# The last product of a seven-product matmul, in column halves on two banks, and the last rows stored in halves

## The chip, the core and the metric

The kernel runs on one core of one Trainium2 chip. The metric is device time in microseconds of one execution; a figure for a kernel is the median of its runs. Five engines work side by side from queues of their own: TensorE (PE; its weight loads are listed as PEld), VectorE (DVE), ScalarE (ACT), GpSimd (POOL) and SyncE (SP), which here issues the stores and the transposing DMAs.

## What is computed

Attention with a sliding window and a linear bias, and behind it a two-layer network with an ELU, in one program:

```python
# q, k, v: (8, 8, 576, 64); w_in: (512, 2048); w_out: (2048, 512)
scores = q @ k^T / 8 - slope[h] * |i - j|     # kept where 0 <= i - j < 128
attn = softmax(scores)
x = (attn @ v) as (4608, 512)                 # tokens x (heads * head_dim)
h = x @ w_in
g = where(h > 0, h, exp(min(h, 0)) - 1)       # ELU
out = g @ w_out                               # (4608, 512), float32
```

## The kernel before

**Stages.** The 4,608 tokens are cut into nine blocks of 512 (`NTB = 9`), and these into 18 pairs `n` of 256 tokens. A schedule written out by hand (`manual_schedule`, slots numbered `s`, dictionaries `early`, `HID`, `tasks`, `OUT`, `late`) fixes the order in which each engine's instructions are issued. In each slot the attention of a later batch, a piece of the hidden layer (`hidden`: 8 matmuls for 256 tokens, two activations on ScalarE; `elu`: one operation on VectorE) and a piece of the output layer follow one another.

**The output layer.** From pair 2 of the 18 on (`SEVEN`, n = 1 to 17) the product of `g` (256 tokens x 2048) with `w_out` (2048 x 512) is not computed as eight block products but as seven, with sums and differences of blocks on VectorE (the scheme of Strassen and Winograd). Rows are cut in two halves of 128, columns in two of 256, the inner dimension in two of 1024. `T[1..4]` are differences of blocks of `w_out`, made once; `sums(n, i)` makes the four sums `S1..S4` of blocks of `g`; `product(n, i)` for i = 1 to 7 is eight accumulating matmuls of 128x128 weights with 256 columns. Products share accumulators in PSUM: of the two banks of a pair, `z` takes 1, then 6, 7 and 4 on top of each other, `x` takes 2 (read together with the copy of product 1), and 5 and then 3. So after product 7 bank `z` holds P1+P6+P7, which ScalarE copies to the SBUF tile `U7` (`kept(n, 7)`), and after product 4 it holds the lower left block of the result.

**Finishing a pair.** `combine` makes three of the four 128x256 blocks with an addition on VectorE (`add`, line 354): C11 is the copy `U1` plus product 2, C12 is `U6` plus product 3 on product 5, C22 is `U7` plus `U5`. The lower left block is bank `z` after product 4, copied by ScalarE (line 398). `put` (line 412) issues the store of a row tile `tile_out(n, i)` (128 rows x 512 columns of float32, tag `ob`) on SyncE's queue: row tile 0 after C12, row tile 1 after C22, 256 KB each.

**The last pair.** n = 17 has no hidden layer beside it any more. Its products run in slots `s = 15 + 8*17` and `s + 1`, with bank `sp2` as `z`, and in the order 1, 2, 6, 5, 7, 3, 4. After product 7 and 3 come C22 (its store takes columns 256 to 512 of row tile 1) and C12 (the store of the whole of row tile 0), then product 4, and then `last_out`: ScalarE copies columns 0 to 128 of bank `sp2` and issues their store on its own queue, VectorE copies columns 128 to 256 and SyncE issues theirs (line 417 the copies, 412 the stores). The banks `hp0` and `hp1`, in which the hidden layer is accumulated, are not used after the last `elu` (line 323).

**Where a store's completion is waited for.** Each store or transposing DMA that SyncE or ScalarE issues counts up one of eight completion semaphores, which are taken in turn. At the end of the program SyncE waits for each of the eight in order of their numbers before the closing barrier.

Of the kernel before, what the change touches and what calls it, by code (L numbers as in the profile page):

```python
# [18 lines left out]
def kernel(  # L19
# [9 lines left out]
    nc = tc.nc  # L29
    B, H, S, D = q.shape  # L30
    NTOK, DO = out.shape
    FF = moe_w_in.shape[1]
    NFC = FF // 128
    NTB = NTOK // 512
# [3 lines left out]
    V = nc.vector  # L38
# [10 lines left out]
    def one(shape, dt, name):  # L49
        return const.tile(shape, dt, name=name, tag=name)  # L50
# [5 lines left out]
    T = [None] + [one([128, 8, 256], F16, f"T{i}") for i in (1, 2, 3, 4)]  # L56
# [21 lines left out]
    hp = [ps_h.tile([128, 512], F32, name=f"hp{i}", tag=f"hp{i}") for i in range(2)]  # L78
# [70 lines left out]
    with tc.manual_schedule():  # L149
# [199 lines left out]
        def A(n, i, k):  # L349
            c = 256 * (n % 2) + 128 * i  # L350
            return gs[n // 2][:, 8 * k:8 * k + 8, c:c + 128]

        def add(o, a, b, op=ALU.add):
            V.tensor_tensor(out=o, in0=a, in1=b, op=op)  # L354
# [16 lines left out]
        def place(n, i):  # L371


            z, x = XY[n] if n < 2 * NTB - 1 else (sp[2], sp[3] if i == 2 else sp[0])
            return (z if i in (1, 4, 6, 7) else x)[:, 0:256]

        def kept(n, i):
            if (n, i) not in U:
                U[n, i] = work.tile([128, 256], F32, name=f"U{i}", tag=f"U{i}", bufs=1)
            return U[n, i]  # L380

        def tile_out(n, i):
            if (n, i) not in obs:
                obs[n, i] = work.tile([128, DO], F32, name="ob", tag="ob")
            return obs[n, i]
# [12 lines left out]
                nc.scalar.copy(tile_out(n, 1)[:, 0:256], o)  # L398

        def combine(n, what):  # L400
            if what == "C11":
                add(tile_out(n, 0)[:, 0:256], kept(n, 1), place(n, 2))
            elif what == "C12":
                add(tile_out(n, 0)[:, 256:512], kept(n, 6), place(n, 3))
                put(n, 0, 0, DO)
            else:
                add(tile_out(n, 1)[:, 256:512], kept(n, 7), kept(n, 5))
                put(n, 1, 0 if n < 2 * NTB - 1 else 256, DO)

        def put(n, i, c0, c1, queue=nc.sync):  # L410
            r = 256 * n + 128 * i
            queue.dma_start(out[r:r + 128, c0:c1], tile_out(n, i)[:, c0:c1])

        def last_out(n):
            o = place(n, 4)
            for c0, copy, queue in ((0, nc.scalar.copy, nc.scalar), (128, V.tensor_copy, nc.sync)):
                copy(tile_out(n, 1)[:, c0:c0 + 128], o[:, c0:c0 + 128])
                put(n, 1, c0, c0 + 128, queue)

        wz = fore[4][:, 0:256]  # L420

# [69 lines left out]
        early, tasks, late, HID, OUT = {}, {}, {}, {}, {}  # L491

        def at(s, f, *a):
            tasks.setdefault(s, []).append((f, a))

        def at_once(s, f, *a):
            tasks.setdefault(s, []).insert(0, (f, a))

        def after(s, f, *a):
            late.setdefault(s, []).append((f, a))  # L500
# [130 lines left out]
        for n in SEVEN:  # L631
            s = 15 + 8 * n
            ps = (19, 20, 21, 22, 23, 25, 27, 29, 30) if n == 1 else range(s, s + 9)
            if n < 2 * NTB - 1:
                for d, i in ((-1, 1), (1, 2), (3, 3), (4, 4)):
                    (at_once if n > 2 else at)(ps[d] if d > 0 else ps[0] - 1, sums, n, i)
                after(ps[2], combine, n, "C11")
                after(ps[6], combine, n, "C12")
                (at_once if n > 2 else at)(ps[8], combine, n, "C22")
                for d in range(8):  # L640
                    OUT[ps[d]] = [(product, (n, i, j, j + 1)) for i, j in turns[7 * d:7 * d + 7]]
            else:
                at_once(s - 3, sums, n, 3)
                for i in (2, 1):
                    at_once(s - 2, sums, n, i, 0, 6)
                    at_once(s - 1, sums, n, i, 6, 8)
                at(s - 1, product, n, 1)
                OUT[s] = [(product, (n, 2)), (combine, (n, "C11")), (sums, (n, 4)), (product, (n, 6)), (product, (n, 5))]
                OUT[s + 1] = [(product, (n, 7)), (product, (n, 3)), (combine, (n, "C22")), (combine, (n, "C12")),
                              (product, (n, 4)), (last_out, (n,))]  # L650


        SOFT = {15 + 8 * n + d for n in SEVEN[1:] for d in (0, 1, 2, 3, 4, 7)} | set(range(11, 19)) | {20, 22, 23} | set(range(16 * NTB - 10, 16 * NTB + 8))
# [45 lines left out]
```

The softmax here doesn't subtract the row's maximum and nothing guards it: scores larger than these inputs give would overflow.

## Time and profile before

| | |
|---|---|
| median of three runs | 311.28 us (310.63 to 312.19) |
| span of the profiled execution, first to last instruction | 308.9 us |
| time of the profiled execution outside its span | not given on the page; the median is 2.4 us above the span |
| granted TensorE clock, mean | 0.998 |
| PE busy | 300.1 us, 97% of the span, 4071 matmuls |
| DVE busy / ACT busy | 257.5 us (83%) / 241.8 us (78%) |
| the chain that ended last: PE / DVE / DMA / ACT / POOL | 72% / 8% / 6% / 5% / 4% |
| stores on SyncE's queue | 35 of 256 KB, 2.2 us from issue to landing (median) |

Times are microseconds from the first instruction. The profile has one row for each instruction; the timeline merges neighbours of one kind, and gives a start, a length, the engine, the line, the operation, the tiles written and read, and in brackets the idle time ahead of it with what ended that. A matmul's end is modelled, and matmuls overlap: the spacing of their starts is what eight of them cost.

### The profile page before, as it was taken

To read this page: it belongs to the slowest core of one execution; us is meant where nothing else is said; L and a number is where in the kernel's file an instruction comes from. 1 tells how busy PE (TensorE), PEld (TensorE's weight loads), DVE (VectorE), ACT (ScalarE), POOL (GpSimd) and SP (SyncE) were. 2 spreads that over 40 slices of the span, in tenths; PEclk is the share of its full clock that TensorE was granted. 3 is DMA by queue.
4 is the path that set the end of the run, shared out by engine and by line. 5 is a ranking of instruction groups with operands and counts; after the bars stand their busy time and mean duration, and the time that the engine had idled before them with its cause. 6 is when DMAs were issued, how large, how long until landed. Compare 5 with 4: busy or idle time off the path is not lost.

```text
span 308.9 us, 9820 instructions
## 1 busy us (share of the span) xinstructions
PE 300.1 (97%) x4071; PEld 256.1 (83%) x4071; DVE 257.5 (83%) x498; ACT 241.8 (78%) x446; POOL 108.4 (35%) x163
## 2 busy tenths in 40 slices
PE   6899999999999999999999999999999999999995
PEld 4788875798888888988888888888899888898884
DVE  4646888988989998997989998989998788886782
ACT  4576678678798788878887889778888897968871
POOL 8937867273252315141616061706000001010000
PEclk9999999999999999999999999999999999999999
DMA  9999999999194919395969896999530202030103
GB/s 96 196 197 202 201 180 185 94 118 115 21 165 63 169 35 161 43 152 59 132 70 138 110 102 78 138 124 122 60 94 7 91 17 87 19 98 0 70 28 110
DMA packets 96509, 32.04 MB, mean 104 GB/s; under 512 B 83920, under 2 KB 91984, under 8 KB 96464
## 3 DMA queue, kind: packets, MB, share of 16 engines
q0 software_dynamic: 75920, 18.36, 64.2%
q1 hardware_dynamic: 20400, 12.98, 17.1%
q8 instruction: 32, 0.52, 0.7%
q14 instruction: 13, 0.11, 0.1%
q10 hardware_dynamic: 144, 0.07, 0.1%
HBM read 36.70 MB, written 9.44 MB: 149 GB/s over the span
## 4 chain that ended last, share of the span: by engine, by line
PE 72%; DVE 8%; DMA 6%; ACT 5%; POOL 4%; issue 4%; POOLq 0%; DVEq 0%
PE hp L305 33%; PE op L393 13%; PE av L393 12%; DMA VP<-in_v_dram 4%; PE spa L225 3%; PE spa L271 3%; DVE g L323 3%; POOL e L316 2%; PE sp L393 2%; ACT e L315 2%; DMA s<-in_q_dram 2%; ACT EX L236 1%; PE sp L253 1%; POOL VP L114 1%; DVE xn L260 1%
## 5 line engine op out<-in xcount | busy, mean ns | idle before, releaser
L305 PE MATMUL hp<-xT,wi 128*128 128x256 f16 (+3 forms) x1488 | 144.2, 245 | 1.0 <-DVE g L323 0.5
L305 PEld LDWEIGHTS <-wi 128*128 128x128 f16 x1600 | 119.9, 98 | 18.1 <-issue 6.3
L323 DVE SCALAR_TENSOR_TENSOR g<-e,hp 128x512 f16<-128x512 f32 x138 | 93.7, 679 | 22.2 <-ACT e L313 12.5
L316 POOL TENSOR_SCALAR e<-e 128x512 f32<-128x512 f32 x44 | 28.0, 636 | 158.8 <-ACT e L315 152.9
L312 ACT ACTIVATE e<-hp 128x512 f32<-128x512 f32 x98 | 58.6, 597 | 28.5 <-PE hp L305 23.1
L313 ACT ACTIVATE e<-e 128x512 f32<-128x512 f32 x100 | 63.1, 631 | 3.2
L393 PEld LDWEIGHTS <-S 128*128 128x128 f16 x544 | 51.2, 98 | 6.7 <-issue 0.6
L393 PEld LDWEIGHTS <-g 128*128 128x128 f16 x408 | 38.2, 98 | 4.7 <-issue 0.6
L241 DVE TENSOR_TENSOR EX<-EX,TAB 128x1024 f16<-128x1024 f16 x48 | 32.9, 686 | 6.2 <-ACT EX L236 4.0
L114 POOL DMA_DIRECT2D VP<-in_v_dram x40 | 34.6, 878 | 0.6 <-PE hp L305 0.3
L315 ACT ACTIVATE e<-hp 128x512 f32<-128x512 f32 x40 | 24.1, 601 | 10.9 <-PE hp L305 10.9
L393 PE MATMUL op<-T,S 128*128 128x256 f16 x200 | 30.0, 273 | 0.1
L233 ACT ACTIVATE EX<-spa 128x1024 f16<-128x1024 f32 x24 | 24.6, 1025 | 3.7 <-PE spa L225 3.4
L393 PE MATMUL av<-T,S 128*128 128x256 f16 x176 | 26.4, 273 | 0.1
L236 ACT ACTIVATE EX<-sp 128x512 f16<-128x512 f32 x48 | 26.0, 596 | 0.0
L354 DVE TENSOR_TENSOR S<-g 128x1024 f16<-128x1024 f16 (+2 forms) x35 | 23.5, 671 | 0.8 <-PE op L393 0.2
L393 PE MATMUL op<-wo,g 128*128 128x256 f16 x128 | 19.2, 272 | 0.1
L393 PE MATMUL av<-wo,g 128*128 128x256 f16 x120 | 18.0, 272 | 0.0
L277 DVE TENSOR_TENSOR xn<-spa,rden 128x512 f16<-128x512 f32 x24 | 16.6, 692 | 0.8
L108 POOL DMA_DIRECT2D st<-in_k_dram x24 | 16.2, 686 | 2.8 <-DMA s<-in_q_dram 1.9
L108 POOL DMA_DIRECT2D st<-in_q_dram x24 | 15.9, 666 | 0.6 <-DMA VP<-in_v_dram 0.6
L271 PE MATMUL spa<-VP,EX 128*128 128x65 f16 x336 | 15.4, 193 | 0.1
(139 smaller groups left out, 379.3 us busy)
## 6 DMA issues: line engine op xcount, KB each, us to landing
out_dram<-ob SPq DMA_DIRECT2D x35, 256.0 KB, 2.2
VP<-in_v_dram POOLq DMA_DIRECT2D x32, 128.0 KB, 5.7
st<-in_k_dram POOLq DMA_DIRECT2D x24, 144.0 KB, 5.2
st<-in_q_dram POOLq DMA_DIRECT2D x24, 144.0 KB, 5.9
wi<-in_moe_w_in_dram POOLq DMA_DIRECT2D x4, 512.0 KB, 10.7
wo<-in_moe_w_out_dram POOLq DMA_DIRECT2D x4, 512.0 KB, 10.1
VP<-in_v_dram POOLq DMA_DIRECT2D x8, 64.0 KB, 5.8
s<-in_k_dram POOLq DMA_DIRECT2D x1, 512.0 KB, 12.1
```

Of the source, the lines that this page charges most:

```text
L108: nc.gpsimd.dma_start(st[b][32 * g:32 * g + 32, w, :, :, :, :].rearrange("p h n j d -> p (h n) (j d)"), (q, k)[w][b, 2 * g:2 * g + 2, :, : ...
L114: nc.gpsimd.dma_start(VP[b % 2][0:p, n, :, 0:D], v[b, :, 128 * n:128 * n + p, :].rearrange("h p d -> p h d"))
L236: nc.scalar.activation(unit(b, u)[:, g, :, :], sp[g].rearrange("p (h c) -> p h c", h=2), AF.Exp, scale=0.125)
L241: V.tensor_tensor(out=e, in0=e, in1=TAB[:, int(u == 3), 2 * gp:2 * gp + 2, :, :], op=ALU.mult)
L271: nc.tensor.matmul(a[:, h // 4, h % 4, :], ex_[u][:, c:c + 128], VP[b % 2][:, n, h, 0:D + 1], start=j == 0, stop=j == len(parts) - 1)
L305: nc.tensor.matmul(p[:, l * w + u0:l * w + u1], w_in_sb[:, c, fc * 128:(fc + 1) * 128], xT[:, c, x0:x0 + u1 - u0], start=(c == 0), stop=(c ...
L312: nc.scalar.activation(e[:, 0:n], p[:, 0:n], AF.Relu, scale=-1.0)
L313: nc.scalar.activation(e[:, 0:n], e[:, 0:n], AF.Exp, scale=-1.0)
L315: nc.scalar.activation(e[:, 0:n], p[:, 0:n], AF.Exp)
L316: nc.gpsimd.tensor_scalar(out=e[:, 0:n], in0=e[:, 0:n], scalar1=1.0, scalar2=0.0, op0=ALU.min, op1=ALU.max)
L323: V.scalar_tensor_tensor(out=gs[t][:, f0:f0 + nf, c0:c0 + w], in0=sh(es.pop((t, c0, f0))), scalar=1.0, in1=sh(hps.pop((t, c0, f0))), op0=A ...
L393: nc.tensor.matmul(o, a[:, j, :], b[:, j, :], start=j == 0 and i in (1, 2, 5), stop=j == 7, skip_group_check=True)
```

## The change

It does three things. First, product 4 of the last pair no longer accumulates on bank `sp2`: it goes to `hp0` and `hp1`, each 128 columns wide, eight matmuls for the first half and then eight for the second. Second, VectorE adds each half to the same columns of `U7`, the copy of P1+P6+P7 that exists for C22 already, and writes the result tile; the first half's store is issued by ScalarE, the second's by SyncE. Third, for the last two pairs (n = 16 and 17, `late`) each 256 KB store is replaced by two of 256 columns, issued as soon as their block is there. The output is the same sum.

```diff
         def combine(n, what):
+            late = n >= 2 * NTB - 2
             if what == "C11":
                 add(tile_out(n, 0)[:, 0:256], kept(n, 1), place(n, 2))
+                if late:
+                    put(n, 0, 0, 256)
             elif what == "C12":
                 add(tile_out(n, 0)[:, 256:512], kept(n, 6), place(n, 3))
-                put(n, 0, 0, DO)
+                put(n, 0, 256 if late else 0, DO)
             else:
                 add(tile_out(n, 1)[:, 256:512], kept(n, 7), kept(n, 5))
-                put(n, 1, 0 if n < 2 * NTB - 1 else 256, DO)
+                if n == 2 * NTB - 2:
+                    put(n, 1, 0, 256)
+                put(n, 1, 256 if late else 0, DO)
...
         def last_out(n):
-            o = place(n, 4)
-            for c0, copy, queue in ((0, nc.scalar.copy, nc.scalar), (128, V.tensor_copy, nc.sync)):
-                copy(tile_out(n, 1)[:, c0:c0 + 128], o[:, c0:c0 + 128])
-                put(n, 1, c0, c0 + 128, queue)
+            for half, queue in enumerate((nc.scalar, nc.sync)):
+                c, o = slice(128 * half, 128 * half + 128), hp[half][:, 0:128]
+                for j in range(8):
+                    nc.tensor.matmul(o, A(n, 1, 1)[:, j, :], T[4][:, j, c], start=j == 0, stop=j == 7)
+                add(tile_out(n, 1)[:, c], kept(n, 7)[:, c], o)
+                put(n, 1, 128 * half, 128 * half + 128, queue)
...
                 OUT[s + 1] = [(product, (n, 7)), (product, (n, 3)), (combine, (n, "C22")), (combine, (n, "C12")),
-                              (product, (n, 4)), (last_out, (n,))]
+                              (last_out, (n,))]
```

## The prediction

> **What bounds the kernel now.** I read the page first. TensorE is busy for nearly the whole span, so work that is moved beside it is worth nothing, except where TensorE has already ended.
>
> ```profile
> span 308.9 us, 9820 instructions
> PE 300.1 (97%) x4071; PEld 256.1 (83%) x4071; DVE 257.5 (83%) x498; ACT 241.8 (78%) x446; POOL 108.4 (35%) x163
> ```
>
> The change touches only the last two pairs, so I went to the end of the chain that ended last (start, length, what):
>
> ```profile
> 303.75 0.87 PE spa L393 x8
> 304.62 0.89 PE sp L393 x8
> 305.51 0.02 issue
> 305.53 0.27 ACT ob L417
> 305.81 0.02 issue
> 305.83 0.29 DVE ob L417
> ```
>
> TensorE leads it up to 305.51. Then the two copies of the last block stand one behind the other, although they are on two engines. The timeline of the same stretch shows why the second is late, and what follows it:
>
> ```profile
> 304.19 0.43 DVE L354 TENSOR_TENSOR ob<-U,U 128x256 f32<-128x256 f32 x1 [1.93 <-ACT U L396]
> 304.46 1.04 PE L393 MATMUL sp<-T,g 128*128 128x256 f16 x8
> 304.64 1.84 SPq L412 DMA_DIRECT2D out_dram<-ob  x3
> 304.66 0.42 DVE L354 TENSOR_TENSOR ob<-U,spa 128x256 f32<-128x256 f32 x1
> 305.53 0.27 ACT L417 COPY ob<-sp 128x128 f32<-128x128 f32 x1 [1.38 <-PE sp L393]
> 305.83 0.37 ACTq L412 DMA_DIRECT2D out_dram<-ob  x1
> 305.83 0.29 DVE L417 COPY ob<-sp 128x128 f32<-128x128 f32 x1 [0.75 <-ACT ob L417]
> ```
>
> VectorE's copy was released by ScalarE's copy (0.75 us idle, "<-ACT ob L417"), not by TensorE: both read bank `sp2`, and the program lets them do so in turn only. SyncE's last store is issued behind VectorE's copy; its row by itself starts at 306.15 and takes 0.33. From there to the end of the span (308.89) are 2.74 us in which no compute engine works. The list of DMAs says that 1.6 of these are that store's way to its landing:
>
> ```profile
> out_dram<-ob SPq DMA_DIRECT2D x1, 64.0 KB, 1.6
> ```
>
> The rest is SyncE's closing waits and the barrier. SyncE's rows for the program's end in the stretch 307.85 to 308.1 are these, the last two lines:
>
> ```profile
> L694 SPq EVENT_SEMAPHORE  x3: 27/28/28, 307.9 to 308.0; - x3
> L694 SPq DRAIN  x1: 13/13/13, 308.1 to 308.1; - x1
> ```
>
> In all there are nine such waits between 306.5 and 308.0. The one at 307.8 is where the last store's landing was noticed; behind it three more semaphores were still looked at, which had long been full, at about 0.06 us each (307.87, 307.93, 307.99), and only then the drain began.
>
> **Product 4 in halves.** It removes 8 matmuls of 256 columns (1.04 us with the last one's 0.272 of latency, so (1.04 - 0.272) / 7 = 0.110 each) and adds 16 of 128 columns, each with a weight load. The same shapes run in the hidden layer early in the trace:
>
> ```profile
> 27.80 0.99 PEld L305 LDWEIGHTS <-wi 128*128 128x128 f16 x17
> 27.86 1.06 PE L305 MATMUL hp<-xT,wi 128*128 128x128 f16 x16
> ```
>
> One such matmul's row is 0.219 long, so the spacing is (1.06 - 0.219) / 15 = 0.056, though a weight load's row is 0.098: consecutive loads overlap. With the first matmul at 304.46 as now, half 0 ends at 304.46 + 7 x 0.056 + 0.219 = 305.07, and half 1 at 304.46 + 15 x 0.056 + 0.219 = 305.52, against 305.50 now: **+0.02**. The banks cost no wait: the last reading of `hp0` is an `elu` that ended at 300.35, and U7's copy (303.79 to 304.16) is over before the product starts. The bounds for the spacing are 0.056 and 0.098 (no overlap of the loads); I take 0.056, since that row has the very shape.
>
> The Trainium skill speaks against this step: its page "TensorE: Matmul & The Clock Gate", section "Back-to-back issue gap", gives a sustained spacing of about 81 ns for a pair of weight load and matmul of 128 columns. By it, as an estimate, half 1 would end 15 x 0.025 = 0.38 us later than in my sum and nearly all of the gain below would go. The trace's sixteen in 1.06 us contradict it here.
>
> **The adds.** Each is a VectorE addition of 128 columns of float32, one operand from PSUM; the trace has none of that size. Above lies the same addition with 256 columns (0.42), below ScalarE's copy of 128 columns (0.27). VectorE's copy of 128 columns out of PSUM is the nearest row, 0.29. Multiplications of float32 from PSUM (L260 and L277 groups) take 0.425 at 256 columns and 0.692 at 512, 1.04 ns a column, and 0.42 - 128 x 0.00104 gives 0.29 again; I take that. Half 0's add is ready at 305.07, as C12's add ends (304.66 + 0.42 = 305.08), runs 305.11 to 305.40, and is covered by half 1 on TensorE; ScalarE's store goes out at 305.43 instead of 305.83. ScalarE now waits for VectorE there, with nothing queued behind it. If the cover were gone (C12's add 0.15 us later), the second add would start to slip.
>
> Half 1's add starts as ScalarE's copy did, 0.03 after TensorE (305.55), for the two halves lie in two banks and, by the program's waits, it waits for TensorE alone; not for half 0's store, though both write one tile. It ends at 305.84, and SyncE issues 0.03 later, at 305.87 instead of 306.15: **-0.28**. SyncE is free then: C12's store is issued at 305.11 as now and takes 0.34. Bounds of this term: -0.30 with an add of 0.27, -0.15 with one of 0.42.
>
> **Stores in halves.** SyncE gets three more issues of 0.33 each. Pair 16's first half goes out after its C11 add (ends at 292.04), its row tile 1 in two issues near 300.7 and 301.4, pair 17's C11 half right behind, near 301.7. SyncE then waits for C22 until 304.64 anyway, with nothing else queued: **0**. The buffer that C22 of pair 17 writes is that of pair 16's row tile 0, whose last half is issued at 299.78 as now and has 4.4 us until 304.19, against 2.2 to land. Without that slack, the C22 add would wait, and C12's store behind it. What changes at the end is that 128 KB fewer are on their way behind 305.1. The last store lands 1.6 us after its issue, like ScalarE's before it, so I see no queueing to save: **0**, with -0.1 as the other end.
>
> **The order of the closing waits.** The three additional DMAs turn the round of eight semaphores by three: by the program's waits the last store, now on the fifth of the eight, gets the eighth. SyncE looks at them in order, so the three looks behind the landing (3 x 0.06) move ahead of it, into time in which it waits anyway: **-0.18**, between -0.18 and 0.
>
> **Sum.** -0.28 - 0.18 = -0.46 against the profiled span, which becomes 308.9 - 0.46 = 308.4 (its TensorE end at 305.52, last issue at 305.87). The 2.4 us outside the span (311.28 - 308.9) are not touched, so the median of the runs goes from 311.28 to 310.82.
>
> **Rivals.** *Half the gain*: the add costs 0.42 as the 256-column one does, or the closing waits stay where they are; then -0.15 - 0.18 = -0.33 or -0.28, that is 310.95 to 311.0. For it speaks that neither row is in the trace.
>
> *Weight loads become the bound* (the slower side): sixteen loads with 128 columns each instead of eight with 256. If at this place a pair takes the 0.098 of a load row, half 1 ends 15 x 0.042 = 0.63 later, and the sum is -0.46 + 0.63 = +0.17, 311.45. It decides from a spacing of 0.056 + 0.46 / 15 = 0.087. Against it are all groups of this shape in the trace, at 0.056 and with TensorE at the same clock.
>
> *The second add waits for the first half's store*, because of the shared result tile. Then it starts at 305.43 + 1.6 = 307.03, the last issue comes at 307.35, and the total is +1.2 - 0.18 = +1.0, 312.3. The listed waits speak against it.
>
> *It doesn't do what it says*: were the end set by another store, nothing would move, 311.28. C12's 256 KB landed 2.0 after 305.11, at 307.1, well ahead of the last one at 307.8, so this is unlikely.
>
> **How the numbers follow.** Forecast (-0.40 to -0.56) 0.60; half the gain 0.20; loads as the bound 0.08; waiting for the store 0.04; nothing moves 0.08. None of the cases reaches 0.5% of the time (1.56 us, about what a measurement of this kernel can tell from no change); such a result would need something that no row here shows, or runs that scatter: the three given lie 0.65 below and 0.91 above their median. I give 0.06 to faster, 0.05 to slower, 0.89 to within. The range goes from 310.82 - 0.65 = 310.2 up past the slower rival (311.45) to 311.7; the store rival at 312.3 is left out, with the tails.
>
> **What would show it.** In the changed profile: sixteen matmuls into `hp` in about 1.06 us from the same distance to C12's add; two adds of 0.29, the first ending before TensorE does, the second 0.03 behind it; SyncE's last issue 0.33 to 0.37 after TensorE's end instead of 0.65; and no look at a semaphore between the last landing and the drain. A spacing over 0.08, an idle time before the second add that ends with a DMA, or a last store that lands in more than 1.8 would each prove me wrong.

## The result and the profile after

The changed kernel takes 310.11 us (median of 16 runs, 309.48 to 310.72). The kernel before, run beside it, takes 310.89 (16 runs, 309.96 to 312.19), 0.39 less than the median of three that the forecast started from. The ratio is 0.9977 (0.9968 to 0.9987): 0.7 us faster, with an interval from 0.4 to 1.0, and within 0.5%. The forecast time of 310.82 was too high, and the measured one lies 0.09 us below the stated range of 310.2 to 311.7. The direction was right, and so was that the change stays within 0.5%; the forecast difference of 0.46 lies in the interval.

The chain that ended last, in the changed kernel (start, length, what):

```profile
304.36 0.87 PE spa L393 x8
305.23 0.91 PE hp L423 x16
306.14 0.02 issue
306.16 0.29 DVE ob L354
```

Where two copies stood in turn there is one addition. The timeline of the same stretch (line 423 are the matmuls in `last_out`, 417 the stores):

```profile
304.80 0.42 DVE L354 TENSOR_TENSOR ob<-U,U 128x256 f32<-128x256 f32 x1 [1.92 <-ACT U L396]
304.96 0.99 PEld L423 LDWEIGHTS <-g 128*128 128x128 f16 x16
305.07 1.06 PE L423 MATMUL hp<-T,g 128*128 128x128 f16 x16
305.27 0.42 DVE L354 TENSOR_TENSOR ob<-U,spa 128x256 f32<-128x256 f32 x1
305.71 0.29 DVE L354 TENSOR_TENSOR ob<-U,hp 128x128 f32<-128x128 f32 x1
306.03 0.37 ACTq L417 DMA_DIRECT2D out_dram<-ob  x1
306.16 0.29 DVE L354 TENSOR_TENSOR ob<-U,hp 128x128 f32<-128x128 f32 x1 [0.16 <-PE hp L423]
```

Sixteen matmuls of 128 columns take 1.06 us, where eight of 256 took 1.04. The first add is done before TensorE ends; the second is released by TensorE (0.16 idle) and by nothing else. SyncE's rows of the program's end, in the stretch 308.02 to 308.2, where before three more looks at semaphores came behind the landing:

```profile
L701 SPq DRAIN  x2: 7/10/13, 308.1 to 308.2; - x2
L701 SPq EVENT_SEMAPHORE  x1: 28/28/28, 308.0 to 308.0; - x1
```

The wait at 308.0 is the one that ends with the last store's landing, and the drain follows at once.

Yet both profiled spans are 308.9 us. The product starts at 304.46 in the one and at 305.07 in the other: this execution of the changed kernel was 0.61 late when it came to the last pair. VectorE's instructions, compared one by one, run within 0.01 of each other up to 4 us, are 0.61 apart at 8.4 us, and 0.61 apart again at the last pair; from 16 us on the distance stays within 0.04 of 0.62, except from 111 to 114 us (up to 0.86). So what the change does is read in the tail, which I measure from the start of C22's add of the last pair to the end of the span, in single rows of the traces. Each figure is from one profiled execution:

| | before | after | difference | forecast |
|---|---|---|---|---|
| product 4's start to the last store's issue | 1.69 | 1.41 | -0.28 | -0.28 |
| issue to the landing noticed | 1.66 | 1.56 | -0.10 | 0 |
| landing noticed to the end | 1.08 | 0.90 | -0.18 | -0.18 |
| C22's add to the end (C22 to product 4 is 0.27) | 4.70 | 4.14 | -0.56 | -0.46 |

### The profile page after: what moved, and what is told of

Its sections match the earlier page's. It is cut to its first block, busy times and chain, and to the rows that moved or that the text cites. A ratio compares the mean times of both kernels' runs of the same rounds, so it can differ in the third digit from the quotient of the medians.

```text
span 308.9 us, 9842 instructions
## 1 busy us (share of the span) xinstructions
PE 300.8 (97%) x4079; PEld 256.5 (83%) x4079; DVE 258.0 (84%) x499; ACT 241.5 (78%) x445; POOL 108.5 (35%) x163
## 4 chain that ended last, share of the span: by engine, by line
PE 76%; DVE 7%; ACT 6%; DMA 5%; issue 3%; POOL 2%; POOLq 0%; DVEq 0%; ACTq 0%
PE hp L305 34%; PE op L393 13%; PE av L393 12%; PE spa L225 4%; PE spa L271 3%; DVE g L323 2%; DMA s<-in_q_dram 2%; DMA VP<-in_v_dram 2%; ACT EX L236 2%; PE op L329 1%; DMA xT<-xn 1%; PE sp L393 1%; POOL e L316 1%; PE sp L305 1%; ACT e L315 1%
## 5 line engine op out<-in xcount | busy, mean ns | idle before, releaser
L393 PEld LDWEIGHTS <-g 128*128 128x128 f16 x400 | 37.4, 98 | 4.6 <-issue 0.6
```

Of the source, the lines that this page charges most:

```text
L393: nc.tensor.matmul(o, a[:, j, :], b[:, j, :], start=j == 0 and i in (1, 2, 5), stop=j == 7, skip_group_check=True)
```

## The experiments

Theory: three separate terms, as in the table. Rivals: the adds carry the whole gain; or the landing term is no term at all, but scatter of one profiled execution. The ratios of the first four are of whole runs, against 35 further runs of the kernel before; their intervals reach half a microsecond and more to each side, so the verdicts rest on the tails, one profile for each run.

### The adds alone

```diff
 # kernel before, with last_out of the changed kernel; puts as before
-                              (product, (n, 4)), (last_out, (n,))]
+                              (last_out, (n,))]
```

> The kernel before with product 4 in halves and the two adds alone; all stores as before. I measure the tail, from the start of C22's add of the last pair to the end of the span: 4.70 us before, 4.14 after (-0.56). First theory, three separate terms (adds -0.28, the round of semaphores -0.18, the landing of the last store -0.10): the adds alone take 0.28 off between product 4's start and the last issue (1.69 to 1.41), the three looks behind the landing stay, and the store lands 1.6 to 1.7 after its issue: tail 4.42, time -0.28. Rival, that the adds carry the whole gain (the last store lands earlier because ScalarE's goes out earlier): tail 4.14 to 4.3, time -0.5 or more.

Measured: ratio 0.998 (0.9964 to 0.9996), tail 4.54. Product 4 to the last issue is 1.41, as forecast, and the three looks behind the landing are still there (1.08 from landing to end). But the landing came 1.78 after the issue. The list of DMAs of the last stretch of this run, and then that of the changed kernel (KB each, issue to landing):

```profile
out_dram<-ob SPq DMA_DIRECT2D x1, 256.0 KB, 2.0
out_dram<-ob ACTq DMA_DIRECT2D x1, 64.0 KB, 2.0
out_dram<-ob SPq DMA_DIRECT2D x1, 64.0 KB, 1.8
```

```profile
out_dram<-ob SPq DMA_DIRECT2D x1, 128.0 KB, 1.7
out_dram<-ob ACTq DMA_DIRECT2D x1, 64.0 KB, 1.7
out_dram<-ob SPq DMA_DIRECT2D x1, 64.0 KB, 1.5
```

Counted from C22's add, the 256 KB of row tile 0 move until 2.59. ScalarE's store is issued at 1.24, and its packets start at 2.44, 1.20 later, where in the changed kernel they start 0.90 after the issue; the last store's start 0.96 later instead of 0.83. Neither theory had this: issued earlier, the last stores run into row tile 0. The whole-run times do not decide here: the interval, 0.1 to 1.1 us faster, holds the theory's 0.28 and the rival's 0.5, and the median of 310.06 is as low as that of the whole change (310.11), though this tail is 0.40 longer.

### The stores in halves alone

```diff
 # changed kernel, with last_out and product 4 of the kernel before
-                              (last_out, (n,))]
+                              (product, (n, 4)), (last_out, (n,))]
```

> The changed kernel with the end of the kernel before: product 4 on the shared bank, two copies in turn; only the stores of the last two pairs are in halves. First theory: product 4's start to last issue stays at 1.69; the last store has the eighth semaphore, so no look lies between landing and drain (-0.18), and with 128 KB fewer on the way it lands 0.10 earlier: tail 4.42, time -0.28. Rival, that the halves of the stores are worth nothing: tail 4.70, time within 0.1.

Measured: ratio 1.0004 (0.9986 to 1.0021), tail 4.43: 1.69 to the issue, 1.58 to the landing, 0.90 to the end. The number is the theory's 4.42; the reason given for 0.10 of it is not, as the next run shows.

### The round of semaphores alone

```diff
 # kernel before
-                put(n, 0, 0, DO)
+                if n == 15:
+                    put(n, 0, 0, 256)
+                put(n, 0, 256 if n == 15 else 0, DO)
...
-                put(n, 1, 0 if n < 2 * NTB - 1 else 256, DO)
+                if n in (14, 15):
+                    put(n, 1, 0, 256)
+                put(n, 1, 256 if n in (14, 15, 17) else 0, DO)
```

> The kernel before with three earlier 256 KB stores (row tile 1 of pair 14, both row tiles of pair 15) issued as two halves one right behind the other, so that the round of eight semaphores turns by three and the last store gets the eighth; everything from pair 16 on as before. First theory: the looks at semaphores behind the landing move ahead of it, tail 4.70 - 0.18 = 4.52, landing as before, time -0.18. Rival, that the order of the looks costs nothing because the barrier waits for something else: tail 4.70, time unchanged.

Measured: ratio 0.9992 (0.9972 to 1.0013), tail 4.43, better than the 4.52 expected. Landing to end is 0.90 (-0.18, as forecast). Here row tile 0 is whole, and yet the last store lands 1.57 after its issue. So 256 KB on the way do not delay a last store that is issued as late as in the kernel before, and the 1.66 of the first profile was not their doing.

### One turn too many

```diff
 # changed kernel: pair 15's row tile 0 in halves as well
-                put(n, 0, 256 if late else 0, DO)
+                if n == 15:
+                    put(n, 0, 0, 256)
+                put(n, 0, 256 if late or n == 15 else 0, DO)
```

> The changed kernel with one more earlier store in halves (row tile 0 of pair 15), so that the last store gets the first of the eight semaphores and ScalarE's the eighth. First theory: SyncE waits for the last landing first and only then looks at the seven others, about 0.06 each: tail 4.14 + 7 x 0.06 = 4.57, time +0.43 against the change, so about -0.13 against the kernel before. Rival (the order costs nothing): tail 4.14, time as with the change.

Measured: ratio 1.0 (0.9979 to 1.002), tail 4.58 (+0.44, forecast +0.43). SyncE's rows in its stretch 307.4 to 308.0:

```profile
L703 SPq EVENT_SEMAPHORE  x8: 28/28/28, 307.4 to 307.9; - x8
L703 SPq DRAIN  x2: 7/10/13, 307.9 to 308.0; - x2
```

The landing is noticed by the first of these eight; the other seven are looked at behind it, one each 0.06 us, and then comes the drain. A store that is split far upstream, whose bytes nobody waits for, takes most of the change's gain away.

### A second base, for repeats

The remaining runs have TensorE transposes and a ScalarE copy in place of SyncE's 31 transposing DMAs. The last pair is the same, and seven early stores are split so that the round of semaphores stands as in the kernel before. Neither the kernel before nor the changed kernel was profiled a second time as it stands.

```diff
 # kernel before
-            if copy is None:
-                nc.sync.dma_start_transpose(out=xT[:, :, o:o + n], in_=x[0:n, :])
-                return
...
-                at(a + 3, turn, b, u)
+                at(a + 3, turn, b, u, nc.scalar.copy, sp[3])
...
+                if 3 <= n < 10:
+                    put(n, 0, 0, 256)
```

> A base for the next runs: the kernel before with its 31 transposing DMAs replaced by TensorE transposes and a ScalarE copy (nothing of it in the last pair), and with seven early stores split, so that the round of eight semaphores stands as before. Its time differs upstream (31 x 4 transposes more on TensorE: some us slower than the kernel before). What counts is the tail, from C22's add of the last pair to the end. If the tail is fixed by the program: 4.70 as before, with the last store landing 1.66 after its issue. Rival, that the landing scatters between executions by some 0.1: 1.57 as in the variants whose last store had the eighth semaphore, tail 4.61.

> The base once more, for the scatter of the tail. The two profiles with this end of the program so far gave 4.70 and 4.62, the whole difference between the last packet of the last store and its landing (0.45 and 0.38). If that part scatters: 4.60 to 4.72 again, product 4 to last issue 1.69 exactly, looks behind the landing three.

> The whole change on the base with TensorE transposes. If the gain is what the tail shows: tail 4.14 (within 0.03), and about 0.56 less time than the base. Rival, that the change also takes something off before the tail: same tail, but 1 us or more less time than the base.

> The change on that base once more: tail 4.14 to 4.20, product 4 to last issue 1.41 exactly, no look behind the landing.

The base takes 375.19 us (373.03 to 377.62), 64 more than the kernel before, where I had written "some us"; why it is so much I did not pursue. With the change it is 373.94 (373.25 to 375.13), 1.25 less; that is what the rival asked for (1 us or more), but with runs of one kernel up to 4.6 us apart it decides nothing about half a microsecond. The tails do: 4.62 and 4.61 for the base, 4.18 and 4.12 with the change. The means differ by 0.47. Term by term: to the last issue 1.69 and 1.69 against 1.41 and 1.41; issue to landing 1.59 and 1.58 against 1.55 and 1.55; landing to end 1.08 and 1.08 against 0.95 and 0.90. In the repeat of the base, the two copies in turn:

```profile
368.60 0.27 ACT L416 COPY ob<-sp 128x128 f32<-128x128 f32 x1 [1.37 <-PE sp L390]
368.90 0.29 DVE L416 COPY ob<-sp 128x128 f32<-128x128 f32 x1 [0.75 <-ACT ob L416]
```

and in the repeat of the change the second add:

```profile
368.23 0.29 DVE L351 TENSOR_TENSOR ob<-U,hp 128x128 f32<-128x128 f32 x1 [0.16 <-PE hp L422]
```

On this base the landing term is thus 0.03, not 0.10. From the last store's last packet to the noticed landing it takes 0.47 and 0.48 in the traces of the kernel before and of the adds alone, and 0.37 to 0.40 in the other nine with a last store of this size on one queue. On the first base the two long ones are the two whose last store has the fifth semaphore, but on the second base the fifth goes with 0.37 and 0.39, so the semaphore alone does not make it. Whether this part scatters between executions or belongs to the program of the first base stays open, and with it 0.07 of the 0.56 in the table.

### Row tile 0 whole

```diff
 # change on the second base; pair 17's row tile 0 in one store behind C12
-                if late:
+                if n == 2 * NTB - 2:
                     put(n, 0, 0, 256)
...
-                put(n, 0, 256 if late else 0, DO)
+                if 3 <= n < 11:
+                    put(n, 0, 0, 256)
+                put(n, 0, 256 if 3 <= n < 11 or n == 16 else 0, DO)
```

> The change on that base, but row tile 0 of the last pair is stored whole (256 KB) behind C12's add as before; one more early store is split, so that the last store keeps the eighth semaphore. First theory: the two last stores meet the 256 KB on the DMA engines, as in the run with the adds alone: ScalarE's packets begin 1.20 instead of 0.90 after their issue, the last store lands 1.70 to 1.78 after its issue instead of 1.56, tail 4.24 to 4.35. Rival, that bytes on the way do not matter: tail 4.14.

Measured: tail 4.24, landing 1.67 after the issue, a little under the 1.70 expected, against 1.55 with the change. The list of DMAs of the last stretch:

```profile
out_dram<-ob SPq DMA_DIRECT2D x1, 256.0 KB, 2.0
out_dram<-ob ACTq DMA_DIRECT2D x1, 64.0 KB, 1.9
out_dram<-ob SPq DMA_DIRECT2D x1, 64.0 KB, 1.7
```

The last two stores' packets start 1.20 and 0.95 after their issues, as with the adds alone. So the halving of row tile 0 keeps 0.12 us of the adds' gain that would otherwise be given back on the DMA engines.

### One add of 256 columns

```diff
 # change on the second base
-            for half, queue in enumerate((nc.scalar, nc.sync)):
-                c, o = slice(128 * half, 128 * half + 128), hp[half][:, 0:128]
...
+            o = hp[0][:, 0:256]
+            for j in range(8):
+                nc.tensor.matmul(o, A(n, 1, 1)[:, j, :], T[4][:, j, :], start=j == 0, stop=j == 7)
+            add(tile_out(n, 1)[:, 0:256], kept(n, 7), o)
+            put(n, 1, 0, 256)
```

> The change on that base with product 4 whole on one free bank (8 matmuls of 256 columns), one add of 256 columns and one store of 128 KB by SyncE, which has the eighth semaphore. First theory: TensorE ends 0.02 earlier, the add takes 0.42 instead of 0.29, the issue comes 0.11 later, and packets of 1 KB take 0.49 instead of 0.34 to move: tail 4.14 + 0.11 + 0.15 = 4.40. Rival, that the halves bring nothing and the gain is that VectorE adds from a bank of its own: tail 4.14 to 4.2.

> The version with one add of 256 columns once more. In its first profile fifteen of sixteen parts of the last store had landed 1.68 after the issue and one part 3.5 after it (tail 6.17). If that was a single late packet: tail 4.37 now. If it belongs to the version: over 5 again.

The first profile gave a tail of 6.17, because one of sixteen parts of the last store landed 3.5 after its issue; the second gave 4.38, where 4.40 and 4.37 were expected. So the delay does not belong to the version, and the two halves are worth 0.23 (4.38 against the mean of 4.15): 0.11 up to the issue, the rest in the larger store's packets (0.48 us from the first to the last). The late part is eight packets that start 4.05 after C22's add, where the others end by 3.11. A 16 KB packet of the queue that the page lists as `instruction` runs from 3.14 to 4.06 there, and in the repeat that queue moves nothing before the landing; that this packet held the late part up fits the times, but no run shows it.

```profile
370.07 0.42 DVE L351 TENSOR_TENSOR ob<-U,hp 128x256 f32<-128x256 f32 x1 [0.45 <-PE hp L421]
```

### The last store on two queues

```diff
 # change on the second base
-                if n == 2 * NTB - 2:
-                    put(n, 1, 0, 256)
-                put(n, 1, 256 if late else 0, DO)
+                put(n, 1, 256 if n == 2 * NTB - 1 else 0, DO)
...
-                put(n, 1, 128 * half, 128 * half + 128, queue)
+                if half == 0:
+                    put(n, 1, 0, 128, queue)
+                else:
+                    for r0, q2 in ((0, nc.sync), (64, nc.scalar)):
+                        r = 256 * n + 128 + r0
+                        q2.dma_start(out[r:r + 64, c], tile_out(n, 1)[r0:r0 + 64, c])
```

> A version past the change, on the base with TensorE transposes: the last half's store goes out as two stores of 64 rows, one by SyncE and one by ScalarE at the same moment, 32 KB each (row tile 1 of pair 16 is stored whole, so that the two last stores have the seventh and eighth semaphore). If the packets of the last store (0.34 us from the first to the last) are what its size costs, half of them on each queue end 0.1 to 0.17 earlier: issue to landing 1.40 to 1.46 instead of 1.55, tail 4.02 to 4.08. Rival, that both queues' packets share the same sixteen engines, or that ScalarE's second issue comes late: tail 4.15 or more.

Measured: tail 4.77, worse by 0.6; the expectation missed. The two stores, issued 0.04 apart, take longer to issue in both queues:

```profile
368.43 0.38 ACTq L414 DMA_DIRECT2D out_dram<-ob  x1
368.87 0.55 SPq L427 DMA_DIRECT2D out_dram<-ob  x1
368.91 0.54 ACTq L427 DMA_DIRECT2D out_dram<-ob  x1
```

The other issues of 64 KB and 128 KB at this place take 0.33 to 0.38. The packets begin 1.19 and 1.44 after the issues, where the last store's begin after 0.83 with the change, and the list of DMAs has the two halves landing 1.9 and 2.1 after their issues, where a store of twice the size takes 1.5:

```profile
out_dram<-ob SPq DMA_DIRECT2D x1, 32.0 KB, 1.9
out_dram<-ob ACTq DMA_DIRECT2D x1, 32.0 KB, 2.1
```

These are also the only stores of 64 rows, all others have 128; whether the moment or the shape makes them slow, no run separates. No version here beat the change.

## Why the prediction was right or wrong

**Product 4 in halves: right.** +0.02 was forecast, and the last matmul of product 4 ends 1.04 after the first one's start before and 1.06 after. The sixteen pairs stand 0.056 apart here too, so the 81 ns of the Trainium skill's page "TensorE: Matmul & The Clock Gate", section "Back-to-back issue gap", do not hold for this stream; by them, as an estimate, the rows would span 15 x 0.081 + 0.219 = 1.43 us. The rival with the weight loads as the bound falls with it.

**The adds: right.** 0.29 each, between the bounds 0.27 and 0.42. What the separate banks remove is the 0.30 us from the start of ScalarE's copy (305.53) to that of VectorE's (305.83); of the 0.75 us that VectorE was idle before it, the other 0.45 went by until TensorE had ended and ScalarE's copy began. The Trainium skill's page "PSUM — Partial Sum Buffer", section "PSUM bank collisions raise a hardware error", says that two engines must not use one bank in the same partitions at once and that the program has to keep them apart; the rows show them kept apart, and no run here shows a collision. The second add did not wait for the first half's store, so that rival falls too.

**Stores in halves: half right.** C22's add still waits for ScalarE's copy of `U7` alone (1.92 us idle, 1.93 before), so the additional issues hold nothing up there, as forecast. But "I see no queueing to save" was true of the kernel before only: with the issues 0.28 to 0.40 earlier, the 256 KB store would have cost 0.12 (row tile 0 whole), and its halving hides that. I had asked what the shorter path triggers on VectorE and SyncE, and not on the DMA engines. That the 0 held for the whole change is luck: the halving that I gave no worth undid a cost that I had not seen.

**The closing waits: right.** -0.18, shown from both sides: by the turn alone (-0.18), and by one turn too many (+0.44 for seven looks).

**What failed is the last step, the sum's base.** I added -0.46 to 311.28, the median of three runs, and took the 2.4 us by which this median lies above the profiled span for time outside the span that stays. The record does not say which of the three runs was profiled, so 2.4 is either a median less another run's span or one unusual run (on the second base three of 28 runs have 2.58 to 2.65). In either case it is not what lies outside the span as a rule. In the sixteen runs of the changed kernel, which have both figures, what lies outside the span is 1.74 to 1.95 us (median 1.79), and in 46 runs of the kernel before, made beside the experiments, 1.74 to 1.91 (median 1.82). The forecast span of 308.4 was nearly right: the median span of the sixteen runs is 308.3. So of the 0.71 between forecast and result, 0.6 is the term outside the span, put at 2.4 where 1.8 was measured, and 0.1 is the span; with 1.8 the sum would have been 310.2. Seen from the runs alone, the median of three was 0.39 above that of sixteen (310.89).

**What stays open.** The whole-run gain, 0.78 between the medians, is 0.32 larger than the forecast 0.46, and larger than the 0.47 and 0.56 of the tails. The interval of 0.4 to 1.0 allows for all of them, and I read the rest as scatter. The two traces show the same instructions at a nearly constant distance from 16 us to the last pair, as said above; the trace of one turn too many, which has the whole change, starts C22's add at 304.19, as the kernel before does; the lowest runs of the two kernels, 309.96 and 309.48, differ by 0.48; and the median of the kernel before itself moves as much from one set of runs to the next: 310.89 in the sixteen, 310.63 in 35 further ones and 311.15 in another ten. But no run shows that the start is the same on average with and without the change, so this part is argued and not shown.

## What to carry to other kernels

Anchor a forecast to the profiled execution's own time, not to the median of others, and find out how far single executions scatter and where, before a range is made narrower than that scatter. At the end of a program, follow the last byte on: which bank the last two readers share, which transfers are still on the way when the last store comes, and what is looked at between its landing and the end. A step that makes the last stores earlier can run them into a transfer that was harmless before.

## What the runs showed of the hardware that was not expected

The executions differ mainly in their first 18 us. TensorE's wait for the second load of `q` (line 136), in the traces of the kernel before, of the stores alone and of the round alone, which are the same programs up to pair 14:

```profile
7.68 0.44 PE L136 MATMUL hp<-ident,s 64*64 64x64 f16 x16 [0.97 <-DMA s<-in_q_dram]
```

```profile
8.64 0.63 PE L136 MATMUL hp<-ident,s 64*64 64x64 f16 x16 [1.83 <-DMA s<-in_q_dram]
```

```profile
6.92 0.44 PE L136 MATMUL hp<-ident,s 64*64 64x64 f16 x16 [0.19 <-DMA s<-in_q_dram]
```

In the second the granted clock fell behind that wait (in the stages row it is the figure after the five engines' busy times):

```profile
8.00:12.00 4.00, 3.36 (x61) 2.90 (x62) 2.06 (x5) 1.33 (x2) 3.56 (x6) 0.56 1.21 166
12.00:18.00 6.00, 5.75 (x86) 4.55 (x85) 3.06 (x10) 3.13 (x7) 3.81 (x11) 0.72 1.35 201
```

and VectorE came 2.67 us late to 17 us and stayed about that late to the end, with a span of 311.2; in the third it was 0.75 early at 17 us, 0.52 early from 40 us on, and the span 308.1. But this one load does not decide the time by itself. In the trace of one turn too many, TensorE gets past it 0.80 earlier than in the kernel before, and then waits for a load of `w_in`:

```profile
6.88 0.44 PE L136 MATMUL hp<-ident,s 64*64 64x64 f16 x16 [0.21 <-DMA s<-in_q_dram]
13.40 1.07 PE L305 MATMUL hp<-xT,wi 128*128 128x128 f16 x16 [1.04 <-DMA wi<-in_moe_w_in_dram]
```

From 16 us on, this execution stays within 0.04 of the kernel before. At 17 us the other five traces on the first base stand between 0.75 early and 2.67 late against that of the kernel before, which is more than the change takes off.
